# The first three second-pass heads one to an iteration, and the go of kept heads in groups of 3 and 3

## The chip, the cores and the metric

The kernel runs on one core of a Trainium2 chip. The metric is the time of one execution on the device in microseconds (us); lower is better. Three runs of the kernel before took 912.86, 911.12 and 912.86 us, a median of 912.86. A core has a matrix engine (TensorE, PE in the profile, its weight loads PEld), a vector engine (VectorE, DVE), a scalar engine (ScalarE, ACT), a general engine (GpSimd, POOL) and a sync engine (SyncE, SP). Here SP issues the loads, POOL the large stores and ACT some other stores. An engine executes its own instructions in the order in which they were written and waits for the others through semaphores.

## What is computed

The reference is one decode step of a transformer block, forward and backward, for B = 2 sequences of one token, model width D = 640, H = 32 heads, a cache of Sk = 4096 positions and head width 128, all in bfloat16:

```
q = layernorm(x) @ wq
p = softmax(q . k_cache * scale);  o = p . v_cache
h = x + o @ wo
out = h + relu(layernorm(h) @ w1) @ w2
```

Besides `out` it returns the gradients of a given `grad_out` by x, k_cache, v_cache, wq, wo, w1 and w2. The two caches have 2 x 32 heads of 1 MB each; both are read, and a gradient of the same size is written for each. The gradient of a V head is the outer product of p and go (go is the gradient by that head's o); the gradient of a K head is the outer product of gs and q, where gs needs go, V and p. So the gradients of a sequence need its forward pass through the MLP and back first, and V is needed a second time.

## The kernel before

**Two passes over the heads.** The order of all work is written out by hand: the program's loops issue instructions in the order in which every engine runs them. The first pass, `p1_iter` (L463), takes the 64 heads (32 of sequence 0, then 32 of sequence 1) in iterations i = 0 to 65. Iteration i transposes K of head i on PE (L416), copies the transposes out of PSUM (L421 on ACT), multiplies by q (L427) and ends in a maximum on DVE (`rmax`, L573). Beside this it multiplies K of head i-1 by its exponentials in two halves on DVE (`pk`, L478), and uses V of head i-2 in eight pieces on PE (`m_ps`, L471). K is given back after the second `pk`, V after the last piece of `m_ps`.

**Middle.** After head 31, `middle_gen` (L733) does sequence 0's attention output, layernorms, MLP and their gradients, in small pieces that run between the steps of first-pass iterations. At its end `go_group` (L672) makes go for a group of heads: one product on DVE for each head (`junk`, L658), then a few small operations on DVE and PE (L681 to L700). The groups stand in `bounds` (L802): for sequence 0, heads 26 and 27, heads 28 to 31, then 0 to 7 and so on.

**Second pass.** `p2_iter` (L837) takes head j of `turns` (L393): of each sequence its kept heads first, those whose V stayed in SBUF (six, heads 26 to 31, of sequence 0, and five of sequence 1), then the others, whose V is loaded again as `Wt` (L458). For a head it transposes V in pairs (L437, copied at L442 on ACT), multiplies by go (L450), writes the gradient of V as two halves (`gV`, L832, its store at L889), and, when the next head starts, gs (`gsp`, L845) and the gradient of K in two halves (`gK`, L832, its store at L870). Both stores are issued by POOL. Before head j starts, `bg_until` (L1058) makes sure that its go is there; if it were not, the rest of that group would be issued in one piece.

**The plan.** `plan` (L1070 to L1078) says which i and which j stand together. The second pass starts at i = P2_AT = 41 and has every second first-pass iteration (41, 43, ... 63), then every one. From i = 66 on it runs alone. In an iteration with both, five of a head's six steps stand between the first pass's steps (`MIXED`, L1120), and the last half of `gV` in the next iteration.

**Tiles of 1 MB.** Twelve tiles in SBUF serve as load targets (`ld`) and as sources of stores (`g`). `give` (L105) returns a tile; with a tag it changes the tile's use. `pump` (L1097) issues the next load of the queue as soon as an `ld` tile is free; which V of the second pass is loaded when follows from the plan (L1090). At i = 41 the tile of K goes from `ld` to `g` (L563), and `give` at L883 hands tiles of kept V to `g` until `g` has three.

Of the kernel before, what the change touches and what calls it, by code (L numbers as in the profile page):

```python
# [15 lines left out]
def kernel(  # L16
# [23 lines left out]
    _, H, Sk, Dh = A_k_cache.shape  # L40
# [64 lines left out]
    def give(t, to=None):  # L105
        tag, k, _ = home_of.pop(id(t))
        to = to or goes_to(tag)
        owned[tag] -= 1
        owned[to] += 1
        free[to] += 1  # L110
        homes[to].append(k)
        given_at[k] = step[0]
# [620 lines left out]
    def middle_gen(b):  # L733
        if o_next[0] < (b + 1) * H // OG:
            o_group()
        nc.vector.tensor_reduce(out=u4[:], in_=u_bank[0][:].rearrange("p (s d) -> p d s", s=4),
                                axis=AX.X, op=ALU.add)
        yield
        while a_next[0] < (b + 1) * H // OG:
            if a_next[0] == o_next[0]:  # L740
                o_group()
                yield
                yield
            a_group()
            yield
        at_bf = small.tile([128, ND], BF16, tag="at_bf", bufs=1, name="at_bf")
        nc.vector.tensor_copy(out=at_bf[:], in_=asum[:, b, :])
        nc.vector.tensor_tensor(out=h1c[:, :, b], in0=xg32[:, b, :], in1=at_bf[:], op=ALU.add)
        h32 = small.tile([128, 1, ND], FP32, tag="h32", bufs=1, name="h32")
        nc.vector.tensor_copy(out=h32[:, 0, :], in_=h1c[:, :, b])  # L750
        yield ("a", b)
        u_out(b)
        yield from ln_fwd(h32[:], 1, x2c[:, :, b:b + 1], rstd2[:, b:b + 1])
        hf_ps = pst([128, NF], FP32, "mid", "hf_ps")
        for cf in range(NF):
            kc = f_kc(cf)
            for c in range(ND):
                nc.tensor.matmul(hf_ps[0:kc, cf:cf + 1], lhsT=w1_t[:, c, cf * 128:cf * 128 + kc],
                                 rhs=x2c[:, c, b:b + 1], start=(c == 0), stop=(c == ND - 1))
            yield 0.25  # L760
        nc.vector.tensor_scalar(out=acol[:, 0:NFF, b], in0=hf_ps[:, 0:NFF], scalar1=0.0, scalar2=None, op0=ALU.max)
        if F_rem:
            nc.vector.tensor_scalar(out=acol[0:F_rem, NFF, b:b + 1], in0=hf_ps[0:F_rem, NFF:NF],
                                    scalar1=0.0, scalar2=None, op0=ALU.max)
        if b == B - 1:
            ar_ps = pst([128, NFF, B], FP32, "mid", "ar_ps")
            for cf in range(NFF):
                for c in range(ND):
                    nc.tensor.matmul(ar_ps[:, cf, :], lhsT=w1_t[:, c, bass.ds(cf, 128, step=NFF)],
                                     rhs=x2c[:, c, :], start=(c == 0), stop=(c == ND - 1))  # L770
                yield 0.25
            nc.vector.tensor_scalar(out=arow[:, 0:NFF, :], in0=ar_ps[:], scalar1=0.0, scalar2=None, op0=ALU.max)
            if F_rem:
                nc.vector.tensor_copy(out=arow[:, NFF, :], in_=acol[:, NFF, :])
        mask = small.tile([128, NF], FP32, tag="mask", bufs=1, name="mask")
        nc.vector.tensor_single_scalar(out=mask[:], in_=acol[:, :, b], scalar=0.0, op=ALU.is_gt)
        nc.vector.tensor_tensor(out=ghfc[:, :, b], in0=ga[:, b, :], in1=mask[:], op=ALU.mult)
        yield from wait(3)
        fbc = cols.tile([128, Dff], BF16, tag="fbc", name="fbc")
        gx2 = small.tile([128, 1, ND], FP32, tag="gx2", bufs=1, name="gx2")  # L780
        gx2p = small.tile([128, ND, 3], FP32, tag="gx2p", bufs=1, name="gx2p")
        FW = Dff // 3
        spread_f = bcast_cols(one(ghfc, b), NF, f_kc, fbc)
        have = 0
        for k in range(3):
            while have < min(Dff, (k + 1) * FW):
                next(spread_f)
                have += 512
                yield
            for c in range(ND):  # L790
                yield from turn()
                ttr(w1_t[:, c, k * FW:(k + 1) * FW], fbc[:, k * FW:(k + 1) * FW], gx2p[:, c, k:k + 1], FW)
                yield 0.85
        nc.vector.reduce_sum(out=gx2[:, 0, :], in_=gx2p[:], axis=AX.X)
        yield ("w1", b)
        yield from ln_bwd(gx2[:], x2c[:, :, b:b + 1], rstd2[:, b:b + 1], gc[:, :, b:b + 1], gh1c[:, :, b:b + 1], 1)
        hbc = cols.tile([128, D], BF16, tag="rowbc", name="hbc")
        yield from bcast_cols(one(gh1c, b), ND, lambda c: 128, hbc)
        yield ("gh1", b)

        first = H - KEPT[b]
        bounds = [(first, first + 2), (first + 2, H)] if b == 0 else [(first, H)]  # L802
        bounds += [(h, min(first, h + GH)) for h in range(0, first, GH)]
        for h0, h1 in bounds:
            yield from go_group(b, h0, h1, hbc)
        if b > 0:
            yield from mlp_out()
# [29 lines left out]
    def p2_iter(j, busy):  # L837

        c = S2[j] if j < NP1 else None
        p = S2[j - 1] if j >= 1 else None  # L840
        if p is not None:
            bp, hp = turns[j - 1]
            pair_matvec(p["dp"], p.pop("T3"), 3, gom[:, hp, bp, :, :])
            gsp = small.tile([128, NSC, 2], BF16, tag="gsp", name="gsp")
            nc.vector.scalar_tensor_tensor(  # L845
                out=gsp[:], in0=p["dp"][:, :, None].to_broadcast([128, NSC, 2]), scalar=negdot[:, hp, bp:bp + 1],
                in1=P_bf[:, bp * H + hp, :, None].to_broadcast([128, NSC, 2]), op0=ALU.add, op1=ALU.mult)
        if c is not None:
            b, h = turns[j]
            go = gom[:, h, b, :, :]  # L850

            bank = pst([128, 512], FP32, "sps", "dp_ps")
            for k, col in enumerate((goc, qsc)):
                nc.tensor.matmul(bank[:, 128 + k * 128:256 + k * 128],  # L854
                                 lhsT=col[:, h, b:b + 1].to_broadcast([128, 128]), rhs=ident_bf[:],
                                 start=True, stop=True)
            c["dp"] = bank[:, 0:NSC]
            rb = mats.tile([128, 256], BF16, tag="rb", bufs=4, name="rb")
            nc.scalar.activation(out=rb[:], in_=bank[:, 128:384], func=ACT.Copy, scale=rt[:, b, h:h + 1])  # L859
            pp = small.tile([128, NSC, 2], BF16, tag="pp", name="pp")  # L860
            nc.gpsimd.tensor_copy(out=pp[:], in_=P_bf[:, b * H + h, :, None].to_broadcast([128, NSC, 2]))
            c.update(rb=rb, pp=pp)
            c["T0"] = pair_transpose(c["W"], 0, busy=busy)
        if p is not None:
            gK = take("g", [128, NSC, 128], "gK")
            outer_half(gK, p["rb"][:, 128:256], gsp, 0)
        yield
        if p is not None:
            outer_half(gK, p["rb"][:, 128:256], gsp, 1)
            nc.gpsimd.dma_start(out=natural(out_2, bp, hp), in_=gK[:])  # L870
            give(gK)
            del S2[j - 1]
        yield
        if c is None:
            return
        c["T1"] = pair_transpose(c["W"], 1, busy=busy)
        pair_matvec(c["dp"], c.pop("T0"), 0, go)
        yield
        c["T2"] = pair_transpose(c["W"], 2, busy=busy)
        pair_matvec(c["dp"], c.pop("T1"), 1, go)  # L880
        yield
        c["T3"] = pair_transpose(c["W"], 3, busy=busy)
        give(c["W"], "g" if j < H and j != 1 and owned["g"] < 3 else None)  # L883
        pair_matvec(c["dp"], c.pop("T2"), 2, go)
        gV = take("g", [128, NSC, 128], "gV")
        outer_half(gV, c["rb"][:, 0:128], c["pp"], 0)
        yield
        outer_half(gV, c["rb"][:, 0:128], c["pp"], 1)
        nc.gpsimd.dma_start(out=natural(out_3, b, h), in_=gV[:])  # L889
        give(gV)  # L890
        yield
# [171 lines left out]
        forced[0] = False  # L1063

    M0_ITERS = 7
    P2_AT = H + 2 + M0_ITERS
    RATES = (0.2, 0.8, 0.2, 0.8, 0.45)
    RATE2 = 0.65
# [2 lines left out]
    i = j = 0  # L1071
    while i <= NP1 + 1 or j <= NP1:
        ii = i if i <= NP1 + 1 else None
        jj = j if i >= NP1 or (i >= P2_AT and (i - P2_AT) % 2 == 0) else None
        plan.append((ii, jj))
        i += 1
        if jj is not None:
            j += 1  # L1078
# [169 lines left out]
```

## Time and profile before

| | |
|---|---|
| median of three runs | 912.86 us (911.12 to 912.86) |
| profiled execution, first to last instruction (span) | 908.6 us |
| time around the span: median less span | 4.26 us |
| PE, DVE, ACT, POOL busy | 740.8, 692.1, 530.7, 173.1 us |
| bytes moved by DMA, mean rate | 363.00 MB, 400 GB/s |
| of these read from HBM, written to it | 212.16 MB, 149.13 MB |
| one load of K or V, issue to landing, median | 16.0 or 15.5 us |
| one store of gV or gK, issue to landing, median | 15.4 or 15.3 us |

The profiled execution has no time of its own beside its span; 4.26 us for what lies around it is the difference from the median. In the page's row of forty slices, a slice is 22.7 us. A row of the view by windows gives, for a stretch of time, the microseconds for which each engine was busy, the granted clock of PE, the mean busy share of the sixteen DMA engines, and the rate at which bytes moved. The timeline gives start and length of single instructions. A DMA's issue has its line on the issuing engine; its landing is a time of its own.

### The profile page before, as it was taken

Reading aid. Unit: us, or ns where it says so; the run is one execution under the profiler, and the core shown is the slowest. Engines: PE = TensorE matmul, PEld = TensorE weight load, DVE = VectorE, ACT = ScalarE, POOL = GpSimd, SP = SyncE. Lnnn points to the kernel's source line nnn. Section 1 sums busy time; section 2 is a strip of 40 time slices with the busy share of each in tenths; the row PEclk is TensorE's granted clock in tenths of the full one; section 3 lists DMA queues with packets and bytes.
Section 4 is the critical chain, followed back from the end, with each engine's and each line's share of the span. In section 5 each row is a group of like instructions: output and inputs, shape, how many; then the busy total and the mean of one; then the engine's idle time right before and its main releaser. Section 6 shows DMA issues by size and latency. Waiting matters only on the chain.

```text
span 908.6 us, 26495 instructions
## 1 busy us (share of the span) xinstructions
PE 740.8 (82%) x11227; PEld 620.3 (68%) x11227; DVE 692.1 (76%) x1282; ACT 530.7 (58%) x1096; POOL 173.1 (19%) x329
## 2 busy tenths in 40 slices
PE   3899999999989898997866844886799778949780
PEld 3788888888878787887765844665667566735560
DVE  2565787877879787786879697986798459899982
ACT  1666665567777777675743443654577656537650
POOL 1232223323201111010011111121222111111120
PEclk9999999999999999898997585655557555555655
DMA  9999999999889999999999999999999999999996
GB/s 364 420 409 404 408 399 409 418 419 362 308 296 339 421 420 423 422 422 420 417 388 406 412 425 413 402 400 392 397 400 389 424 425 425 423 427 425 425 422 261
DMA packets 56262, 363.00 MB, mean 400 GB/s; under 512 B 5680, under 2 KB 11696, under 8 KB 15312
## 3 DMA queue, kind: packets, MB, share of 16 engines
q1 hardware_dynamic: 34704, 212.18, 57.9%
q0 software_dynamic: 18432, 134.23, 35.6%
q10 hardware_dynamic: 3008, 14.91, 4.1%
q8 instruction: 88, 1.44, 0.6%
q14 instruction: 30, 0.25, 0.1%
HBM read 212.16 MB, written 149.13 MB: 398 GB/s over the span
## 4 chain that ended last, share of the span: by engine, by line
PE 36%; DMA 27%; DVE 18%; ACT 9%; issue 7%; POOL 0%; SPq 0%; POOLq 0%; ACTq 0%; DVEq 0%
DMA out_dram<-gK 11%; DMA Vt<-in_A_v_cache_dram 10%; PE m_ps L471 9%; PE t_ps L416 8%; PE t_ps L437 6%; DVE gV L832 5%; ACT t_sb L421 4%; DVE gK L832 4%; PE s_ps L427 4%; DVE junk L658 3%; PE u_ps L500 3%; DMA wqs<-in_A_wq_dram 3%; DMA out_dram<-gV 2%; DVE pk L478 2%; DMA Kt<-in_A_k_cache_dram 2%
## 5 line engine op out<-in xcount | busy, mean ns | idle before, releaser
L421 ACT COPY t_sb<-t_ps 128x1024 bf16<-128x1024 bf16 x223 | 217.8, 1018 | 45.6 <-PE t_ps L416 45.3
L442 ACT COPY t_sb<-t_ps 128x512 f32<-128x512 f32 x256 | 149.8, 588 | 132.0 <-PE t_ps L437 128.9
L478 DVE TENSOR_TENSOR pk<-Kt,ep 128x2048 bf16<-128x2048 bf16 x128 | 156.3, 1221 | 57.9 <-ACT ep L526 29.1
L437 PE MATMUL t_ps<-ident_f,Wt 128*128 128x128 f32 x848 | 190.9, 371 | 1.0 <-ACT t_sb L421 1.0
L471 PE MATMUL m_ps<-pk,Vt 128*128 128x129 bf16 x2048 | 171.3, 222 | 11.7 <-DMA Vt<-in_A_v_cache_dram 10.3
L832 DVE TENSOR_TENSOR gK<-rb,gsp 128x2048 bf16<-128x2048 bf16 x128 | 152.5, 1225 | 22.2 <-DMA out_dram<-gV 20.4
L832 DVE TENSOR_TENSOR gV<-rb,pp 128x2048 bf16<-128x2048 bf16 x128 | 153.0, 1219 | 20.9 <-DMA out_dram<-gK 18.0
L416 PE MATMUL t_ps<-ident_bf,Kt 128*128 128x128 bf16 x2048 | 152.3, 223 | 8.2 <-DMA Kt<-in_A_k_cache_dram 2.3
L437 PEld LDWEIGHTS t_ps<-ident_f,Wt 128*128 128x128 f32 x848 | 131.4, 191 | 32.4 <-issue 26.1
L471 PEld LDWEIGHTS <-Vt 128*128 128x128 bf16 x2048 | 125.0, 99 | 41.4 <-issue 30.0
L416 PEld LDWEIGHTS <-Kt 128*128 128x128 bf16 x2048 | 125.2, 100 | 16.3 <-issue 10.4
L450 PEld LDWEIGHTS <-t_sb 128*128 128x128 bf16 x2048 | 95.7, 106 | 44.4 <-issue 18.8
L450 PE MATMUL dp_ps<-gom,t_sb 128*128 128x2 bf16 x2048 | 95.1, 167 | 9.2 <-ACT t_sb L442 8.0
L488 POOL COPY pk<-ep 128x16 bf16<-128x16 bf16 x80 | 64.9, 812 | 188.2 <-ACT ep L526 159.9
L427 PE MATMUL s_ps<-qc,t_sb 128*128 128x1 bf16 x2048 | 88.1, 164 | 1.6 <-DVE t_sb L419 0.8
L889 POOL DMA_DIRECT2D out_dram<-gV x64 | 34.3, 536 | 277.0 <-DVE gV L832 198.3
L870 POOL DMA_DIRECT2D out_dram<-gK x64 | 34.1, 533 | 253.6 <-DVE gK L832 196.5
L427 PEld LDWEIGHTS <-t_sb 128*128 128x128 bf16 x2048 | 77.5, 97 | 4.4 <-ACT t_sb L421 1.2
L942 ACT CAST ot<-o_ps 128x512 bf16<-128x512 f32 (+4 forms) x160 | 70.3, 489 | 13.7 <-DMA out_dram<-ot 9.3
L859 ACT ACTIVATE rb<-dp_ps,rt 128x256 bf16<-128x256 f32 x64 | 30.4, 476 | 59.8 <-PE dp_ps L854 58.5
L585 ACT CAST MT<-m_ps 128x128 bf16<-128x128 f32 x64 | 17.1, 268 | 72.8 <-PE m_ps L471 72.7
L658 DVE CUSTOM_DVE_ANT_0 junk<-wo_t,hbc 128x640 bf16<-128x640 bf16 x64 | 52.4, 818 | 0.2
(197 smaller groups left out, 781.0 us busy)
## 6 DMA issues: line engine op xcount, KB each, us to landing
Kt<-in_A_k_cache_dram SPq DMA_DIRECT2D x64, 1024.0 KB, 16.0
Vt<-in_A_v_cache_dram SPq DMA_DIRECT2D x64, 1024.0 KB, 15.5
out_dram<-gV POOLq DMA_DIRECT2D x64, 1024.0 KB, 15.4
out_dram<-gK POOLq DMA_DIRECT2D x64, 1024.0 KB, 15.3
Wt<-in_A_v_cache_dram SPq DMA_DIRECT2D x53, 1024.0 KB, 14.0
wq_t<-in_A_wq_dram SPq DMA_DIRECT2D x5, 1024.0 KB, 8.9
wo_t<-in_A_wo_dram SPq DMA_DIRECT2D x4, 1280.0 KB, 18.7
wqs<-in_A_wq_dram SPq DMA_DIRECT2D x5, 1024.0 KB, 17.2
```

The lines of the kernel that those rows point to most:

```text
L416: nc.tensor.transpose(t_ps[:, j, :], nat[:, g * GT + j, :], ident_bf[:])
L421: nc.scalar.copy(out=t_sb[:], in_=t_ps[:])
L427: nc.tensor.matmul(dst[:, sc:sc + 1], lhsT=t_sb[:, j, :], rhs=vec, start=True, stop=True)
L437: nc.tensor.transpose(t_ps[:, j, :], natf[:, 2 * cc:2 * cc + 2, :].rearrange("p c k -> p (c k)"), ident_f[:])
L442: nc.scalar.copy(out=t_sb[:], in_=t_ps[:])
L450: nc.tensor.matmul(dst[:, sc:sc + 2], lhsT=v[:, j, :, par], rhs=vecs[:, par, :], start=(par == 0), stop=(par == 1))
L471: nc.tensor.matmul(r["m"][:, 0:129], lhsT=r["V"][:, sc, :], rhs=r["pk"][sc // HALF][:, sc % HALF, 0:129], start=(sc == 0), stop=(sc == NSC ...
L478: nc.vector.tensor_tensor(out=p["pk"][k][:, :, 0:128].rearrange("p s (a two) -> p s a two", two=2), in0=p["K"][:, sl, :].rearrange("p s (a ...
L488: nc.gpsimd.tensor_copy(out=col, in_=e)
L658: nc.vector.tensor_tensor_reduce(out=junk[0:kc, 0:width], in0=in0, in1=in1, scale=1.0, scalar=0.0, op0=ALU.mult, op1=ALU.add, accum_out=acc)
L832: nc.vector.tensor_tensor(out=pairs_view(dst[:, sl, :]), in0=row.rearrange("p (a two) -> p a two", two=2)[:, None, :, :].to_broadcast([128 ...
L942: nc.scalar.copy(out=ot[0:P, k, n0:n0 + nn], in_=o_ps[0:P, 0:nn])
```

## The change

The plan gets a constant RAMP = 3: the second pass also runs at i = 42. Its heads stand at i = 41, 42, 43, 45, 47, ... 63, then at every i, so that before i = 66 it has begun fifteen heads (j = 0 to 14) instead of fourteen; the plan has 116 iterations instead of 117. The first two go groups of sequence 0 become heads 26 to 28 and 29 to 31. In `p2_iter` the head whose kept V does not go to `g` is j = 2 instead of j = 1.

```diff
@@ middle_gen @@
         first = H - KEPT[b]
-        bounds = [(first, first + 2), (first + 2, H)] if b == 0 else [(first, H)]
+        bounds = [(first, first + 3), (first + 3, H)] if b == 0 else [(first, H)]
@@ p2_iter @@
         c["T3"] = pair_transpose(c["W"], 3, busy=busy)
-        give(c["W"], "g" if j < H and j != 1 and owned["g"] < 3 else None)
+        give(c["W"], "g" if j < H and j != 2 and owned["g"] < 3 else None)
@@ plan @@
     M0_ITERS = 7
+    RAMP = 3
     P2_AT = H + 2 + M0_ITERS
...
-        jj = j if i >= NP1 or (i >= P2_AT and (i - P2_AT) % 2 == 0) else None
+        jj = j if i >= NP1 or (i >= P2_AT and ((i - P2_AT) % 2 == 0 or i < P2_AT + RAMP)) else None
```

## Prediction

> **What bounds the kernel now.** I read the forty slices first, then the place of the change in windows of 5 us, then its iterations, then single issues.
>
> ```profile
> DMA  9999999999889999999999999999999999999996
> GB/s 364 420 409 404 408 399 409 418 419 362 308 296 339 421 420 423 422 422 420 417 388 406 412 425 413 402 400 392 397 400 389 424 425 425 423 427 425 425 422 261
> ```
>
> The rate says more than the busy share: most slices move 400 to 427 GB/s, so for most of the span the kernel waits for bytes. The exception is slices 9 to 12 (204 to 295 us), at 296 to 362. The second pass starts inside them: the first rb (L859) stands at 265.4 us. By windows of 5 us:
>
> ```profile
> 270.00:275.00 5.00, 4.95 (x98) 4.63 (x95) 4.34 (x8) 3.62 (x9) 0.00 (x0) 1.00 0.60 192
> 275.00:280.00 5.00, 4.55 (x93) 3.92 (x90) 4.90 (x15) 4.24 (x9) 1.69 (x2) 1.00 0.80 285
> 280.00:285.00 5.00, 4.22 (x79) 3.58 (x79) 4.36 (x10) 4.18 (x9) 0.53 (x1) 1.00 0.97 387
> 285.00:290.00 5.00, 4.82 (x102) 4.67 (x100) 3.82 (x10) 2.74 (x7) 0.00 (x0) 1.00 1.00 365
> 290.00:295.00 5.00, 5.00 (x99) 4.28 (x97) 5.00 (x12) 4.05 (x10) 1.70 (x2) 1.00 0.96 333
> 295.00:300.00 5.00, 3.03 (x59) 2.81 (x58) 3.16 (x6) 3.27 (x8) 0.00 (x0) 1.00 1.01 416
> 300.00:305.00 5.00, 4.34 (x84) 3.80 (x83) 3.17 (x6) 2.88 (x6) 0.53 (x1) 1.00 1.01 421
> ```
>
> The last column fills up at 295 us. Against 421 GB/s the four rows from 275 to 295 lack 136, 34, 56 and 88 GB/s: 314 x 5 us = 1.57 MB, or 3.7 us of transfer. The same iterations (41, 42, 43 and 44, cut near their rmax) and two later stretches:
>
> ```profile
> 264.00:272.00 8.00, 7.07 (x126) 6.11 (x125) 4.28 (x12) 5.92 (x12) 0.00 (x0) 1.00 0.73 275
> 272.00:278.00 6.00, 5.95 (x120) 5.13 (x119) 6.00 (x10) 5.43 (x13) 1.69 (x2) 1.00 0.79 283
> 278.00:287.00 9.00, 7.77 (x159) 7.01 (x156) 7.46 (x20) 6.60 (x13) 0.53 (x1) 1.00 0.97 366
> 287.00:295.00 8.00, 7.82 (x152) 6.96 (x149) 7.62 (x20) 6.04 (x14) 1.70 (x2) 1.00 0.98 336
> 690.00:890.00 200.00, 159.58 (x1440) 116.91 (x1438) 162.16 (x231) 120.23 (x255) 31.69 (x68) 0.57 1.01 422
> 300.00:450.00 150.00, 133.69 (x2437) 118.32 (x2436) 117.89 (x238) 107.18 (x221) 16.44 (x27) 0.94 1.01 422
> ```
>
> Up to 295 us the engines bound it (iteration 42 has DVE busy all 6.00 of 6.00 us and PE 5.95); from 300 on the bytes do, at 422 GB/s in both long stretches. So I count in two currencies: before 295 us an instruction costs time, after it a byte does. The stores and loads concerned:
>
> ```profile
> 275.36 0.69 POOL L889 DMA_DIRECT2D out_dram<-gV  x1 [13.49 <-DVE gV L832]
> 282.82 0.53 POOL L870 DMA_DIRECT2D out_dram<-gK  x1 [5.78 <-DVE gK L832]
> 291.74 0.53 POOL L889 DMA_DIRECT2D out_dram<-gV  x1 [8.38 <-DVE gV L832]
> 300.46 0.53 POOL L870 DMA_DIRECT2D out_dram<-gK  x1 [7.02 <-DVE gK L832]
> ```
>
> They landed 5.2, 8.1, 10.2 and 8.9 us after issue. The rmax of iterations 40 to 45 start at 263.6, 271.6, 278.4, 287.3, 294.6 and 304.4 us: an iteration with a second-pass head lasts 8.0 (i = 41) or 8.9 us (43), one without 6.8 (42) or 7.3 (44).
>
> **What the change moves.** No operation on a head goes away; one more head stands before i = 45. Head 1 runs in iteration 42 instead of 43, head 2 in 43 instead of 45, and every later one a place earlier. When the full stretch begins, 2 x 1.049 MB of stores more are under way. At 421 GB/s that is 4.98 us of later transfer time: the **credit**. It can't exceed what the holes have room for, 3.7 us, plus what a late first pass opens.
>
> **Cost 1, the head's work in iteration 42.** On DVE it brings gsp 0.28, two gK of 1.225 and, of its gV, nearly one half more than before. Next to each other in the timeline such instructions take less than their length: from the start of a gV to its successor is 1.14 us, from a junk of 0.82 to its reader 0.74. Iteration 42 would hold two gV halves 2.28, one junk with its reader 0.9, nb 0.2, gsp 0.3, two gK 2.3, two pk 2.3 and rmax, OU and OFc 0.3: 8.6 us in place of 6.8. Rows of mixed iterations give 8.0 and 8.9, so 1.2 to 2.1 more; I take 1.8. PE gets 16 transposes (4 pieces of 0.66) and 4 pieces of 0.34 for the products, about 4 us; it was full too, and both run in parallel. Iterations 43 and 44 keep the same load with another head: nothing.
>
> **Cost 2, a new wait of DVE for a tile.** With one head after the other, the two g tiles come round at once. Stepping through take and give: gV of head 0 uses K's tile, gK of head 0 the first kept V; gV of head 1 takes K's again, gK of head 1 the first V's again, since the tile that head 1 hands over stands behind them. By the sums above, gV of head 0 is issued near 275.1 and its tile wanted near 280.2; landing after 5.2 us it is free. gK of head 0 is issued near 277.9 and its tile wanted near 283.8; landing after 5.2 to 8.1 us it comes free at 283.1 to 286.0. The wait is 0 to 2.2 us; I take the middle, 1.1. Behind the waiting gK in DVE's queue stand both pk of iteration 43, behind them on SP the next load of K, and on PE m_ps. If all landed after 10.2 us the waits would add up to some 7 us.
>
> **Costs at nothing.** The group of three go has one more junk (0.82 us) before i = 41; it takes the place of one of the second group, and stepping through the loop shows each group of sequence 0 finished in an earlier iteration than the head that needs it. The second (heads 29 to 31) and the third (0 to 7) are done just in the iteration before; that is the cover, and without it up to three junks, 2.5 us, would go out in one piece. Loads: the three g tiles are complete at i = 42 instead of 45, and head 2 returns its tile to ld instead; counting the tiles that come free, the loads issued by the end of i = 44 are the same number and at i = 45 one more. SP has its first V of the second pass a place earlier among K and V; POOL has the same sequence of stores. The middle of sequence 1 starts at the same i and is always ahead of its heads; the end is byte-bound (421 GB/s and a store landing 14.7 us after issue), which hides that the last gradient work stands one head nearer the end.
>
> **Sum.** Credit 4.98 - 1.8 - 1.1 = 2.1 us, with ends 4.98 - 1.2 = 3.7 (also the whole hole) and 4.98 - 2.1 - 2.2 = 0.7. The profiled span of 908.6 would become 906.5; with the 4.26 us between span and median, **910.8 us** against 912.86.
>
> **Two rules against it.** POOL's gK and gV are issued while DVE is busy; the store issued at 291.74, in a window with DVE busy 5.00 of 5.00, landed after 10.2 us, the one at 275.36 after 5.2, so a busy DVE alone does not decide. The Trainium skill (SBUF — State Buffer, summary of rules for kernel authors) says that descriptor generation for stores from GpSimd starves while VectorE runs in its fast modes. By that rule the stores of heads 0 and 1 would come only with DVE's next pause, and the credit would shrink to about nothing. The same section tells to reckon with some 358 GB/s for HBM. By that figure the rows at 285 and 333 alone lack anything, 0.5 MB or an estimated 1.4 us as a bound; the rows at 421 and 422 contradict it here.
>
> **Rivals.** *The waits win (slower).* If gV and gK of head 1 wait more than 3.2 us together, slip exceeds credit. With gV waiting 5.1 us (a landing of 10.2 instead of 5.2, wanted 5.1 us after its issue) the slip is 6.9 and the time 914.8. For it: landings of 8 to 10 us right after. Against it: at 278 only one load is outstanding. *The gain is given back.* The stretches 450 to 460, 460 to 470 and 485 to 490 run at 368, 390 and 344 GB/s, holes of 3.0 us where the passes part; with another head there they may grow by two thirds: 912.9. *The head is free.* The second pass alone takes (884.5 - 485.1) / 48 = 8.3 us a head and the plan has one iteration less; if only the 1.8 us of iteration 42 were paid, 906.4. Against it: 422 GB/s from 300 to 450 us leaves no room for the shifted bytes.
>
> **Chances.** Forecast 0.50, of which 0.32 lie over 0.2% (1.8 us, about what a measurement can tell from no change) below before; waits 0.22; given back 0.18; free 0.10. So faster 0.42, same 0.36, slower 0.22. The range from 906.8 to 915.2 takes in the forecast's ends and the waits' price; it leaves out most of the free head and waits beyond 5.5 us.
>
> **What would show it.** After: rmax of iteration 42 near 280 and of 45 near 307 us; windows from 280 to 295 at 400 or more; gK of head 1 waiting for out_dram on DVE 0 to 2 us; 422 still from 300 to 450; rb of head 12 some 4 us before its 459.4 us, since it stands at i = 63 then. Wrong: windows from 280 to 300 as empty as before, waits of DVE over 3 us there, or a lower rate after 450 us.

## The result, and the profile after

The changed kernel takes **918.04 us** (median of 11 runs, 915.67 to 922.44) against 912.86 (median of 11 runs, 910.53 to 915.50): a ratio of 1.0059, 95% interval 1.0043 to 1.0075. It is slower, where 910.8 was forecast. The profiled execution has a span of 914.5 us (908.6 before). Its own time is 916.29 us.

The page's rows of forty slices, now 22.9 us each:

```profile
DMA  9999999999779999999999999999989999999997
GB/s 365 420 409 403 408 402 409 419 415 369 291 279 376 371 424 422 422 420 423 422 401 362 422 422 423 420 388 382 394 340 366 424 425 417 424 423 425 425 424 303
```

Slices 9 to 12 (counted from 0) stood at 362, 308, 296 and 339 before and at 369, 291, 279 and 376 now. They are hardly fuller, the next slice fell from 421 to 371, and there is a hole that was not there: the thirtieth figure, 340, and the 366 behind it (663 to 709 us; 400 and 389 before). Four stretches by windows show how much each weighs; the last column is GB/s. First the kernel before:

```profile
270.00:320.00 50.00, 44.82 (x867) 40.03 (x865) 41.45 (x84) 36.88 (x77) 6.70 (x9) 1.00 0.94 367
320.00:650.00 330.00, 257.81 (x3800) 223.45 (x3798) 265.20 (x496) 185.63 (x392) 49.92 (x96) 0.77 1.01 411
650.00:710.00 60.00, 52.67 (x499) 39.96 (x498) 51.78 (x87) 41.74 (x94) 14.85 (x24) 0.61 0.99 397
710.00:880.00 170.00, 135.50 (x1173) 97.85 (x1172) 139.29 (x193) 101.16 (x216) 26.12 (x56) 0.54 1.01 425
```

The same windows of the changed kernel:

```profile
270.00:320.00 50.00, 43.88 (x808) 38.97 (x801) 40.42 (x78) 34.55 (x73) 7.77 (x11) 0.97 0.91 344
320.00:650.00 330.00, 251.24 (x3833) 217.17 (x3832) 263.95 (x487) 183.05 (x387) 50.55 (x94) 0.80 1.01 412
650.00:710.00 60.00, 47.58 (x457) 36.96 (x456) 47.53 (x83) 35.64 (x83) 10.56 (x22) 0.55 0.91 358
710.00:880.00 170.00, 135.98 (x1228) 97.02 (x1226) 138.08 (x191) 105.70 (x230) 27.18 (x56) 0.59 1.01 423
```

Both kernels move 363.00 MB. At the place of the change the kernel now moves (367 - 344) x 50 = 1.15 MB less, 2.7 us at 421 GB/s; it should have moved more. From 650 to 710 us it lacks another (397 - 358) x 60 = 2.34 MB, 5.6 us, 350 us away from the change. The two other rows differ by 0.8 us each, in opposite directions. Part of the 8.3 us comes back behind 880 us, where the old kernel moved only 294 GB/s and the new one 344; 5.9 us of span remain. So there are two losses to explain, a **near** one and a **late** one.

The near one by windows of 5 us:

```profile
270.00:275.00 5.00, 4.97 (x98) 4.46 (x91) 3.44 (x6) 2.87 (x8) 0.00 (x0) 1.00 0.29 74
275.00:280.00 5.00, 4.18 (x80) 3.38 (x78) 4.97 (x7) 4.59 (x10) 2.03 (x3) 1.00 0.84 349
280.00:285.00 5.00, 4.97 (x96) 4.73 (x94) 4.51 (x10) 3.19 (x7) 0.00 (x0) 1.00 0.98 352
285.00:290.00 5.00, 4.22 (x78) 3.50 (x77) 4.96 (x8) 3.86 (x9) 2.02 (x3) 1.00 0.99 393
290.00:295.00 5.00, 4.95 (x110) 4.70 (x108) 3.86 (x10) 3.48 (x9) 0.00 (x0) 1.00 1.02 411
295.00:300.00 5.00, 4.62 (x87) 3.83 (x84) 4.79 (x16) 3.32 (x9) 1.49 (x2) 1.00 1.01 351
300.00:305.00 5.00, 1.38 (x20) 1.32 (x21) 1.35 (x5) 1.50 (x3) 0.00 (x0) 0.91 0.99 403
305.00:310.00 5.00, 5.00 (x78) 4.43 (x77) 3.40 (x5) 3.82 (x8) 0.53 (x1) 0.74 1.01 419
310.00:315.00 5.00, 4.96 (x99) 4.63 (x97) 4.27 (x8) 3.69 (x9) 0.00 (x0) 1.00 1.00 375
315.00:320.00 5.00, 4.62 (x93) 4.00 (x91) 4.87 (x13) 4.22 (x9) 1.71 (x2) 1.00 0.95 310
```

The hole of before, 275 to 295 us, is partly filled: 349, 352, 393 and 411 against 285, 387, 365 and 333, together 0.68 MB more. But 270 to 275 us fell from 192 to 74, and 295 to 300 us and 310 to 320 us are new holes. Between 300 and 305 us PE and DVE are busy for 1.4 of 5 us each: something holds both.

The starts of rmax give the length of each first-pass iteration (us):

| iteration | 40 | 41 | 42 | 43 | 44 | 45 | 46 | rmax 45 starts at |
|---|---|---|---|---|---|---|---|---|
| before | 7.0 | 8.0 | 6.8 | 8.9 | 7.3 | 9.9 | 6.8 | 304.4 |
| after | 7.2 | 9.2 | 9.3 | 9.7 | 6.9 | 12.9 | 6.8 | 311.6 |

By these lengths the first pass loses 0.2 us in iteration 40, 1.1 in 41, 2.5 in 42, 0.8 in 43, -0.4 in 44 and 3.1 in 45, 7.3 us in all (by the starts before rounding). The stores came earlier by 4.98 us of transfer. The difference, 2.3 us, is close to the 2.7 of the windows. The link between the two is argued: a first pass that is late by so much gives its tiles back late, and its loads are issued late.

What holds PE and DVE in iteration 45 stands in the chain of waits (start, us, what; one part of it):

```profile
291.73 0.51 PE t_ps L437 x4
...
292.26 10.93 DMA Vt<-in_A_v_cache_dram
...
303.24 0.64 PE m_ps L471 x8
```

PE's last transpose of a kept V sets a tile free at 292.24, the load of V of head 43 goes into it, lands 10.93 us later, and m_ps had waited for it. Before, the same link reads:

```profile
287.79 8.79 DMA Vt<-in_A_v_cache_dram
```

The wait was there already (PE's timeline of the kernel before):

```profile
296.63 0.64 PE L471 MATMUL m_ps<-pk,Vt 128*128 128x129 bf16 x8 [1.60 <-DMA Vt<-in_A_v_cache_dram]
```

Now the load is issued 4.5 us later and takes 2.1 us longer, and PE waits 3.37 us. The wait is not the whole of it. Behind it PE's granted clock is lower: 0.74 (the third figure from the end) from 305 to 310 us in the windows above. In the kernel before (first row) it is 1.00 there, in a second execution of the changed kernel (second row) 0.50:

```profile
305.00:310.00 5.00, 4.95 (x96) 4.12 (x93) 5.00 (x10) 4.97 (x11) 1.71 (x2) 1.00 1.01 426
305.00:310.00 5.00, 4.62 (x58) 4.50 (x57) 3.84 (x5) 2.48 (x6) 0.53 (x1) 0.50 0.97 403
```

At the lower clock PE takes longer for the same work: four transposes of V last 1.06 us at 304.60 against 0.60 at 297.93 before. So of the 3.1 us more in iteration 45, 1.8 are the longer wait and the rest comes behind it. The first theory was therefore: *the near loss is engine work plus a contention of that load with the stores of heads 1 and 2*; its rival, *the wait of DVE for store tiles*. For the late loss: *what is switched on j now comes an iteration too early*, against *it follows from the near loss*, since a later first pass makes everything later.

### The profile page after: what moved, and what is told of

Its sections match the earlier page's. It is cut to its first block, busy times and chain, and to the rows that moved or that the text cites. A ratio compares the mean times of both kernels' runs of the same rounds, so it can differ in the third digit from the quotient of the medians.

```text
span 914.5 us, 26491 instructions
## 1 busy us (share of the span) xinstructions
PE 733.3 (80%) x11227; PEld 612.4 (67%) x11227; DVE 692.1 (76%) x1282; ACT 527.6 (58%) x1096; POOL 174.9 (19%) x329
## 2 busy tenths in 40 slices
DMA packets 56262, 363.00 MB, mean 397 GB/s; under 512 B 5680, under 2 KB 11696, under 8 KB 15312
## 4 chain that ended last, share of the span: by engine, by line
PE 38%; DMA 26%; DVE 19%; ACT 9%; issue 7%; SPq 0%; POOL 0%; ACTq 0%; POOLq 0%; DVEq 0%
DMA Vt<-in_A_v_cache_dram 12%; PE m_ps L471 9%; PE t_ps L416 8%; PE t_ps L437 7%; DVE gV L832 5%; DVE gK L832 5%; DMA wqs<-in_A_wq_dram 4%; ACT t_sb L421 4%; DMA out_dram<-gK 4%; DMA out_dram<-gV 4%; PE s_ps L427 4%; DVE junk L658 3%; PE u_ps L500 3%; DVE gxj L658 2%; PE o_ps L936 2%
## 5 line engine op out<-in xcount | busy, mean ns | idle before, releaser
L437 PE MATMUL t_ps<-ident_f,Wt 128*128 128x128 f32 x848 | 184.9, 361 | 2.6 <-ACT t_sb L421 2.6
L437 PEld LDWEIGHTS t_ps<-ident_f,Wt 128*128 128x128 f32 x848 | 127.2, 186 | 37.1 <-issue 30.6
L942 ACT CAST ot<-o_ps 128x512 bf16<-128x512 f32 (+4 forms) x160 | 70.2, 491 | 20.5 <-DMA out_dram<-ot 14.1
## 6 DMA issues: line engine op xcount, KB each, us to landing
out_dram<-gV POOLq DMA_DIRECT2D x64, 1024.0 KB, 12.9
out_dram<-gK POOLq DMA_DIRECT2D x64, 1024.0 KB, 12.9
Wt<-in_A_v_cache_dram SPq DMA_DIRECT2D x53, 1024.0 KB, 14.6
```

What stands on the lines that cost most here:

```text
L437: nc.tensor.transpose(t_ps[:, j, :], natf[:, 2 * cc:2 * cc + 2, :].rearrange("p c k -> p (c k)"), ident_f[:])
L942: nc.scalar.copy(out=ot[0:P, k, n0:n0 + nn], in_=o_ps[0:P, 0:nn])
```

## The experiments

Each line is a ratio of times to the kernel before, measured beside it on the same chip, with its 95% interval; behind it the rates (GB/s) of its one profiled execution in the two stretches. "Later" means that both switches on j described below come one head later.

| kernel | ratio | 270 to 320 us | 650 to 710 us |
|---|---|---|---|
| before | 1 | 367 | 397 |
| the change | 1.0059 (1.0043 to 1.0075) | 344 | 358 |
| the change again | 1.0085 (1.0060 to 1.0110) | 334 | 373 |
| e1 the change, later | 1.0062 (1.0039 to 1.0085) | 339 | 387 |
| e2 before, switches one head earlier | 1.0034 (1.0016 to 1.0053) | 367 | 378 |
| e3 before, go groups 3 and 3 | 1.0020 (1.0004 to 1.0036) | 351 | 389 |
| e4 before, one more head at i = 54 | 1.0039 (1.0019 to 1.0059) | 366 | 365 |
| e5 the change, head 1's tile to ld | 1.0084 (1.0059 to 1.0110) | 328 | 368 |
| e7 before, later | 1.0005 (0.9982 to 1.0027) | 368 | 403 |
| e8 the change, four stores left out | one run, 915.68 us | 300 | 366 |
| e9 before, q tiles later | 1.0007 (0.9983 to 1.0031) | 363 | 399 |
| e10 e4, later | 1.0005 (0.9978 to 1.0031) | 361 | 397 |
| e11 the change, later, q tiles later | 1.0066 (1.0042 to 1.0091) | 340 | 389 |
| e12 before, one more head at i = 44, later | 1.0011 (0.9988 to 1.0035) | 352 | 399 |
| e13 the change, later, groups 2, 1 and 3 | 1.0068 (1.0044 to 1.0092) | 334 | 386 |
| e15 e4, rates later only | 0.9993 (0.9977 to 1.0010) | 367 | 387 |
| e16 e4, hand-over later only | 1.0012 (0.9995 to 1.0030) | 369 | 389 |

Single executions of one kernel differ by several us (before: 908 to 918), so ratios carry the verdicts, and a trace is read for what stands at its place in all of them.

**The change again.** No edit; it shows which parts of the difference repeat.

> The changed kernel once more, to see which holes of its trace come back. Keyed theory (the later background work is switched by the head's number j, so a second pass that is one head ahead gets its slow background rate and its tile hand-over one plan iteration earlier, and the stretch with few load tiles lasts longer): about 918 us, the load queue again stands still for some 45 us around 655 to 700 us, against 38 us before, and the windows from 660 to 700 us run near 350 GB/s. Rival (the weak stretch at 660 to 700 us was chance of one execution): about 918 us, but the hole stands elsewhere or is gone in this trace.

Both losses repeat. The lengths of iterations 41 to 44 are the same to 0.1 us; iteration 45 lasts 15.2 instead of 12.9 us, with a load of V of 12.10 us, a wait of 3.51 and the clock of 0.50 shown above. The late loss is there too (373 for 397). Iteration 45 is the one of these lengths that differs between executions: in the four traces with the changed kernel's heads, go groups and tiles (the two, e1 and e11) it lasts 12.9, 15.2, 14.6 and 13.8 us, in the eight with the old ones (the kernel before, e2, e4, e7, e9, e10, e15, e16) 9.1 to 11.9. By the means, 14.1 and 10.0, it costs 4.1 us; the pair of traces read above shows less.

### The near loss

**e3: the go groups alone.**

```diff
-        bounds = [(first, first + 2), (first + 2, H)] if b == 0 else [(first, H)]
+        bounds = [(first, first + 3), (first + 3, H)] if b == 0 else [(first, H)]
```

> The kernel before with only the go groups of 3 and 3 (heads 26 to 28, 29 to 31). Theory: the third go ahead of the first second-pass head delays iteration 41 by about 1.1 us in the stretch that the engines bound, so 913.5 to 914.2 us, rmax of iteration 41 near 272.7 us. Rival as predicted blind (hidden): 912.9 us, rmax of 41 at 271.6 us.

It costs 0.20% (0.04 to 0.36), 1.8 us. Iteration 41 lasts 9.2 us, as in the changed kernel, with nothing else of the change there. PE's timeline of e3 (start, us, engine, line; in brackets the idle time before and what ended it):

```profile
263.93 0.34 PE L427 MATMUL s_ps<-qc,t_sb 128*128 128x1 bf16 x8
265.48 0.35 PE L688 MATMUL d_ps<-pr,ones_f32c 128*128 128x3 f32 x2 [1.21 <-DVE gom L342]
265.69 0.21 PE L692 MATMUL d_ps<-goc,MT 128*128 128x1 bf16 x3
```

Before, the product at L688 had no wait, with 2 columns for two heads:

```profile
262.59 0.36 PE L688 MATMUL d_ps<-pr,ones_f32c 128*128 128x2 f32 x2
```

The third junk makes DVE reach the group's small operations later, and PE, which executes in order, stands 1.21 us at d_ps with the transposes of the next first-pass head behind it. So the third go, costed at nothing, costs the whole of iteration 41's slip.

**e13: the first group of two kept, then one, then three** (on e1).

```diff
-        bounds = [(first, first + 3), (first + 3, H)] if b == 0 else [(first, H)]
+        bounds = [(first, first + 2), (first + 2, first + 3), (first + 3, H)] if b == 0 else [(first, H)]
```

> The changed kernel with the switches on j one head later, and the go of kept heads in groups of 2, 1 and 3 (heads 26 and 27, 28, 29 to 31): head 28 is done in iteration 41 or 42, so no third go stands in front of the first second-pass head, and the ramp is kept. Theory (the third go costs 1.2 us of iteration 41): iteration 41 lasts 8.0 us, 915.5 to 917 us against 917 to 918.5 with three. Rival (the wait moves to another iteration): iteration 41 lasts 8.0, but 42 or 43 is longer by as much, and the time is as with groups of 3 and 3.

No gain: the small operations then run once more. Iteration 41 lasts 10.4 us (42: 8.9, 45: 15.0), and now DVE waits for PE:

```profile
272.14 0.16 DVE L694 TENSOR_SCALAR negdot<-d_ps 128x1 f32<-128x1 f32 x1 [3.01 <-PE d_ps L692]
```

With one group more in this stretch there is one wait more, whatever the number of heads in it.

**e8: the four stores of heads 1 and 2 left out** (on the changed kernel; everything else stays).

```diff
+            if j - 1 not in (1, 2):
-            nc.gpsimd.dma_start(out=natural(out_2, bp, hp), in_=gK[:])
+                nc.gpsimd.dma_start(out=natural(out_2, bp, hp), in_=gK[:])
...
+        if j not in (1, 2):
-        nc.gpsimd.dma_start(out=natural(out_3, b, h), in_=gV[:])
+            nc.gpsimd.dma_start(out=natural(out_3, b, h), in_=gV[:])
```

> The changed kernel without the four stores of second-pass heads 1 and 2 (4.2 MB of the gradients of K and V are not written); nothing else is left out. Only iterations 42 to 46 are read from it. Theory (the loads of K and V lose the transfer to these stores): iteration 45 takes 9 to 10 us instead of 12.9 to 15.2, and PE does not wait for V there. Rival (loads are late because their tiles come free late): iteration 45 still 12 us or more.

Iterations 42 and 43 last 9.3 and 9.7 us as with the stores; these are engine work. Iteration 45 lasts 8.7 instead of 12.9 us. PE's timeline of the changed kernel:

```profile
299.66 0.22 PE L517 MATMUL s_ps<-neg_ident,rmax 128*128 128x128 bf16 x1
303.24 0.64 PE L471 MATMUL m_ps<-pk,Vt 128*128 128x129 bf16 x8 [3.37 <-DMA Vt<-in_A_v_cache_dram]
```

The same place in e8, whose first pass runs 1.3 us later as a whole:

```profile
300.58 0.22 PE L517 MATMUL s_ps<-neg_ident,rmax 128*128 128x128 bf16 x1
300.79 0.64 PE L471 MATMUL m_ps<-pk,Vt 128*128 128x129 bf16 x8
```

Without the stores PE does not wait for V, though the load (at 293.59) is issued as late against its iteration as in the changed kernel: it landed within 7.2 us, by the m_ps at 300.79, where it took 10.93. The clock stays at 1.00. That the wait in iteration 45 comes from a load slowed beside these stores is shown in this one execution, which is shorter there than any other. It leaves out four stores, two more than the change brings in. What it brings to the end is little: 4.2 MB fewer are 10.0 us at 421 GB/s, the one run took 915.68 us, 2.4 under the changed kernel's median. In its trace 650 to 710 us runs at 366 again. As far as one run can tell, bytes saved here are not worth their transfer time at the end.

**e5: head 1 gives its tile back to ld and head 2 to g** (the third edit of the change undone).

```diff
-        give(c["W"], "g" if j < H and j != 2 and owned["g"] < 3 else None)
+        give(c["W"], "g" if j < H and j != 1 and owned["g"] < 3 else None)
```

> The changed kernel with the condition j != 1 kept, so that the V tile of the second kept head goes back to the loads and that of the third to the stores. The load of V that iteration 45 waits for then has a tile some 1.7 us earlier. Theory (iteration 45 waits for V because its load is issued too late): iteration 45 takes 10 to 12 us instead of 12.9 to 15.2, 915 to 917 us. Rival (it is late because the stores of heads 1 and 2 share the transfer with it): iteration 45 as long as before, 918 us. Second rival (with two store tiles, gV of head 2 waits for a store to land): DVE waits for out_dram 1 to 3 us in iteration 43 or 44.

The load of V goes out earlier, at 290.70 instead of 292.26, but now g lacks a tile, and DVE waits (timeline of e5):

```profile
296.48 1.23 DVE L832 TENSOR_TENSOR gV<-rb,pp 128x2048 bf16<-128x2048 bf16 x1 [4.38 <-DMA out_dram<-gV]
```

Iteration 44 grows from 6.9 to 12.6 us, and 45 shrinks from 12.9 to 10.4. A ratio of 1.0084 (1.0059 to 1.0110) is no better than the changed kernel's. The wait moved to the other kind of tile. This is the mechanism of the rival "the waits win"; the third edit of the change keeps it out.

**e12: one more head at i = 44, old go groups, later** (the kernel before, with this edit and the three edits of e7 below).

```diff
-        jj = j if i >= NP1 or (i >= P2_AT and (i - P2_AT) % 2 == 0) else None
+        jj = j if i >= NP1 or (i >= P2_AT and ((i - P2_AT) % 2 == 0 or i == P2_AT + 3)) else None
```

> The extra head at i = 44 instead of 42 (second-pass heads at i = 41, 43, 44, 45, 47, ...), with the go groups of 2 and 4 of the kernel before, and the switches on j one head later. Iteration 41 then lasts 8.0 us again (no third go in front of it). Theory (local sum: credit 4.98 us against the head's work of some 2.5 us and a longer wait for V): cumulative bytes at 330 us within 2 us of transfer of before, better than the changed kernel by 1.4 us or more; time 912 to 915 us. Rival (the burst of stores always ends in a late load of V): rmax of iteration 46 still 4 us or more behind, and bytes at 330 us 2 to 4 us behind.

The lead is the same, two iterations later, and no loss can be measured (1.0011, 0.9988 to 1.0035). Iterations 41 to 43 have their old lengths, 44 lasts 9.8 (7.3 before), 45 15.3 us. That long iteration has the other cause: DVE waits for a store to land, and with it nb and all that stands behind.

```profile
302.77 1.23 DVE L832 TENSOR_TENSOR gV<-rb,pp 128x2048 bf16<-128x2048 bf16 x1 [4.27 <-DMA out_dram<-gV]
```

So a third head inside these iterations stalls either PE for V or DVE for a tile, wherever it is put. Against e1 (1.0062) it saves the go group's 1.1 us and some engine work. But its first pass is 7.9 us late behind iteration 45, counted from the rmax of 40, against 7.1 in the changed kernel and 8.7 in e1, as its rival had it. So the lateness of the first pass does not by itself give the time, and why e12 is 0.5% better than e1 stays open.

### The late loss

In the second pass alone the program reads j in two places. The pace at which the middle of sequence 1 runs beside the heads falls from 0.8 to 0.45 after j = H, with fewer slots a head; and from j = H + KEPT[1] - 1 the large tiles are handed over to g, q and f (`share`, at L1147 and L1148 of the kernel before). With one head more begun, both come one iteration of the plan earlier, while the middle itself is started by i. Stepping through the loop shows load tiles down to five for five iterations of the plan (91 to 95) instead of three (92 to 94).

**e2 and e7: the kernel before, with the switches one head earlier and one later.** e2:

```diff
-        elif fin is not None and j >= H + KEPT[1] - 1:
+        elif fin is not None and j >= H + KEPT[1] - 2:
...
-                      2 if i is not None else 3 if j <= H else 4]
+                      2 if i is not None else 3 if j <= H - 1 else 4]
...
-                slot[0] = int(k in ((1, 3, 5) if j <= H else (1, 4)))
+                slot[0] = int(k in ((1, 3, 5) if j <= H - 1 else (1, 4)))
```

> The kernel before, its plan untouched, with the same three switches one head earlier (j <= H - 1, hand-over from j = 35). Keyed theory: slower by some 5 us, 917 to 919 us, with the load queue still for some 45 us. Rival (the loss comes from the ramp or from chance): 912.9 us.

> The kernel before, its plan untouched, with the three switches on j one head later than they are (both j <= H become j <= H + 1, hand-over from j = 37). Keyed theory, if a later switch goes on helping: 910 to 912 us, windows from 660 to 710 us at 400 GB/s or more. If before already has the best place: 912 to 914 us.

e7 has `j >= H + KEPT[1]` and `j <= H + 1` (twice) at the same places. Earlier costs 0.34% (0.16 to 0.53) with no change at all near 300 us; later changes nothing (0.9982 to 1.0027). A loss there does not need the near one. Five load tiles last five iterations of the plan in e2, as in the changed kernel, and two in e7.

**e4, e10, e15, e16: a lead of one head without the near stretch.** e4 puts one more head at i = 54, into the 422 GB/s; the others undo one or both switches on top of it.

```diff
-        jj = j if i >= NP1 or (i >= P2_AT and (i - P2_AT) % 2 == 0) else None
+        jj = j if i >= NP1 or (i >= P2_AT and ((i - P2_AT) % 2 == 0 or i == P2_AT + 13)) else None
```

> The kernel before with one more second-pass head, but at i = 54, in the stretch that runs at 422 GB/s, and with its own go groups: the lead of one head without the ramp near 300 us. Keyed theory (a lead of one head alone costs later, through the switches on j, and in a full stretch it buys nothing): 915 to 917 us, windows from 660 to 710 us at 355 to 380 GB/s instead of 397, nothing lost before 450 us. Rival (the loss is all in the ramp): 912 to 913 us.

> The run with the extra head at i = 54, and now also the switches on j one head later. Keyed theory: of the 3.9 us that the lead of one head cost there, most comes back: 912 to 913.5 us, windows from 660 to 710 us at 389 to 400 GB/s instead of 359. Rival (the lead costs elsewhere, where the two passes part): still 915 us or more, 660 to 710 us full again and 450 to 510 us at 384 GB/s instead of 401.

> The run with the extra head at i = 54, with only the background's rate and slots switched one head later; the hand-over of tiles stays at j = 36. If the slower go is what the lead costs: 912 to 913.5 us and windows from 660 to 710 us at 385 to 400 GB/s. If the hand-over is: 915 us and 360 GB/s as without it.

> The run with the extra head at i = 54, with only the hand-over of tiles one head later; rates and slots switch as in it. If the hand-over is what the lead costs: 912 to 913.5 us and windows from 660 to 710 us at 385 to 400 GB/s. If the slower go is: 915 us and 360 GB/s as without it.

e10 has e7's three edits, e15 only the two with `j <= H + 1`, e16 only `j >= H + KEPT[1]`. The lead costs 0.39% with the switches coupled to it, and nothing that can be measured with them moved: 1.0005, 0.9993 and 1.0012, intervals within 0.9977 to 1.0031. Moving either switch alone seems enough. For the rates (e15) no loss is left; for the hand-over (e16) this is less certain, since its interval (0.9995 to 1.0030) overlaps e4's (1.0019 to 1.0059). Stepping through the loop, five load tiles last five iterations in e4, four in e15 and e16, three in e10. The window from 660 to 710 us of e4:

```profile
660.00:710.00 50.00, 44.11 (x409) 33.91 (x407) 39.64 (x68) 32.71 (x76) 8.32 (x19) 0.54 0.89 359
```

The same of e10, both switches moved:

```profile
660.00:710.00 50.00, 45.46 (x446) 36.02 (x446) 44.27 (x75) 34.88 (x80) 12.73 (x21) 0.59 1.00 399
```

Of e15, the rates alone:

```profile
660.00:710.00 50.00, 45.28 (x422) 34.22 (x421) 45.72 (x76) 34.53 (x80) 11.68 (x21) 0.59 0.96 385
```

And of e16, the hand-over alone:

```profile
660.00:710.00 50.00, 44.69 (x428) 35.38 (x425) 42.91 (x72) 34.48 (x78) 12.30 (x21) 0.57 0.98 388
```

e4 shows the changed kernel's hole (357 in the same 50 us there) at full size, with the near stretch untouched (366 for 367 GB/s from 270 to 320 us). DVE does fewer operations (68 instead of 72 to 76), and the DMA engines are busy for 0.89 of the time. The lead itself, taken where the rate was full already, buys nothing that can be measured either: 0.9993 (0.9977 to 1.0010) is the best of the four, and of all kernels here. No version tried is faster than the kernel before. (e10's profiled execution took 918.99 us, its median is 911.81; its trace is read for this stretch only.)

**e1: the change with both switches later.**

```diff
-        elif fin is not None and j >= H + KEPT[1] - 1:
+        elif fin is not None and j >= H + KEPT[1]:
...
-                      2 if i is not None else 3 if j <= H else 4]
+                      2 if i is not None else 3 if j <= H + 1 else 4]
...
-                slot[0] = int(k in ((1, 3, 5) if j <= H else (1, 4)))
+                slot[0] = int(k in ((1, 3, 5) if j <= H + 1 else (1, 4)))
```

> The changed kernel with the three switches that look at j moved one head on (both j <= H become j <= H + 1, the tile hand-over starts at j = 37), so that they come at the same plan iteration as before the change. Keyed theory: the 5 to 6 us lost between 660 and 710 us come back and the local loss of 2 to 3 us near 300 us stays: 912 to 914 us; load queue still for some 38 us. Rival (chance, or the head lead itself): 918 us as without it. Rival (all of the loss is the ramp near 300 us): 918 us.

The hole is mostly gone from the trace (387 GB/s from 650 to 710 us instead of 358 and 373), the time is not: 1.0062 (1.0039 to 1.0085) against 1.0085 (1.0060 to 1.0110) for the changed kernel beside it and 1.0059 in the first measurement. The intervals overlap; a recovery of 0.3% is neither shown nor excluded. So in the changed kernel itself the switches have not been shown to be the larger part. In e1's execution the near stretch was also among the worse ones (iteration 45 took 14.6 us, and 339 GB/s).

**e9 and e11: the q tiles later**, on the kernel before and on e1. The queue of loads (SP) stands still in this stretch, and a hand-over that leaves more tiles to ld first should shorten it.

```diff
-            share(ld=5 + more, g=5 + 2 * more, f=3, q=2 + 3 * more)
+            share(ld=7 - more, g=5 + 2 * more, f=3, q=5 * more)
```

> The kernel before with one change in the hand-over of tiles from j = 36 on: the loads keep 7 tiles instead of 5 until all go of sequence 1 are made, and the q tiles, which nothing uses before that, come only then. Theory (the weak stretch from 660 to 700 us comes from loads that stand still for want of tiles): the load queue stands still for 15 to 25 us instead of 38 us, windows from 660 to 710 us at 405 GB/s or more, 909.5 to 911.5 us against 912 to 913. Rival (the stretch is bound by the work on DVE and PE beside it, the loads only follow): rate and time as before.

> The changed kernel with the switches on j one head later and the hand-over of the q tiles only when all go are made. Theory: nothing is left lost after 650 us; what stays are the 2 to 5 us near 300 us and what the parting of the passes takes: 914 to 916 us. Rival: 917 us or more, as with the switches alone.

The waits of SP's queue from 620 to 720 us (us in total, times, longest), first in the kernel before:

```profile
SPq L458 <- PE t_ps L437: 74.2, 5, 37.9
```

In the changed kernel:

```profile
SPq L458 <- PE t_ps L437: 91.6, 6, 44.7
```

In e9:

```profile
SPq L458 <- PE t_ps L437: 46.3, 5, 12.3
SPq L458 <- PE dp_ps L450: 38.4, 3, 22.3
```

The longest standstill grew from 37.9 to 44.7 us with the change, which looked like the cause. e9 cuts it to 22.3, and neither the rate (399 for 397) nor the time (1.0007, 0.9983 to 1.0031) follows; e11 (longest standstill also 22.3 us) stays at 1.0066. So the standstill of before costs nothing that can be measured. Whether the longer one causes the hole is not tested: e9 and e11 start from kernels that do not have the hole, or hardly, and no run gives e4 or the changed kernel more load tiles. In e15 the standstill is 42.3 us, at 387 GB/s and without a loss.

## Why the prediction was wrong, point by point

**What bounds the kernel: right up to 450 us, and read too short.** Up to 295 us engines, from 300 to 450 bytes, held. But in the old kernel PE already waited 1.60 us for V in iteration 45, on a load that took 8.79 us. The prediction read this iteration's end (304.4) and not what it waited for.

**Credit, 4.98 us: the stores came, their worth did not.** Windows from 280 to 295 us were to be at 400 or more and are at 352, 393 and 411; 0.68 of the missing 1.57 MB were filled. The ceiling "the hole, plus what a late first pass opens" was in the text; the sum took all of the 4.98 all the same. It also priced a byte moved early at its full transfer time up to the end; in e8's one run 10.0 us of bytes fewer brought 2.4.

**Cost 1, 1.8 us in iteration 42: mis-sized, and it ended too early.** It measured 2.5 us. DVE's timeline of the changed kernel (the iteration reaches from 272.78 to 282.05):

```profile
272.89 1.23 DVE L832 TENSOR_TENSOR gV<-rb,pp 128x2048 bf16<-128x2048 bf16 x1
274.03 0.82 DVE L658 CUSTOM_DVE_ANT_0 junk<-wo_t,hbc 128x640 bf16<-128x640 bf16 x1
...
274.77 1.22 DVE L832 TENSOR_TENSOR gV<-rb,pp 128x2048 bf16<-128x2048 bf16 x1
...
276.42 2.46 DVE L832 TENSOR_TENSOR gK<-rb,gsp 128x2048 bf16<-128x2048 bf16 x2
278.81 1.21 DVE L478 TENSOR_TENSOR pk<-Kt,ep 128x2048 bf16<-128x2048 bf16 x1
...
282.05 0.19 DVE L573 TENSOR_REDUCE rmax<-s_ps 128x1 bf16<-128x32 f32 x1 [0.46 <-PE s_ps L427]
...
284.04 1.22 DVE L832 TENSOR_TENSOR gV<-rb,pp 128x2048 bf16<-128x2048 bf16 x1
```

The parts are those of the prediction's list, nearly back to back as it said. What it left out are the 0.46 us for PE at the end and the small copy of P_bf. **"Iterations 43 and 44 keep the same load: nothing" failed**: both halves of a head's gV come behind the next rmax. Iteration 43 of before held no gV, since 42 had no head; now it holds two (282.16 and 284.04), 2.3 us, and loses the end of a go group and a wait of 0.56. It is 0.8 us longer.

**Cost 2, the wait of DVE for a tile: did not occur.** From 264 to 320 us DVE waits for no out_dram. POOL's timeline of the changed kernel:

```profile
276.31 0.69 POOL L889 DMA_DIRECT2D out_dram<-gV  x1 [14.38 <-DVE nb L519]
...
279.19 0.53 POOL L870 DMA_DIRECT2D out_dram<-gK  x1 [1.39 <-DVE gK L832]
...
285.55 0.53 POOL L889 DMA_DIRECT2D out_dram<-gV  x1 [5.83 <-DVE nb L519]
...
288.42 0.53 POOL L870 DMA_DIRECT2D out_dram<-gK  x1 [1.38 <-DVE gK L832]
```

They landed after 4.4, 5.6, 8.3 and 8.9 us. gK of head 1 started at 285.69, behind the landing of head 0's gK at 284.8. So the rival "the waits win" had the sign, by luck: its time (914.8) was 3.2 us short, and its mechanism did not occur; e5 and e12 show that it stood one tile or one iteration away (4.38 and 4.27 us).

**"Costs at nothing: the third go junk" failed.** Finished in time was the wrong question; PE's in-order wait behind it (1.21 us) is what costs, 1.1 us in iteration 41 and 0.20% alone (e3).

**"Costs at nothing: loads" failed in iteration 45.** The count of loads up to iteration 44 was right (eight from 263 us on, in both traces); but the one that PE waits for goes out later by the slip and lands later beside two heads' stores, and PE runs at a lower clock behind the wait: 3.1 us more in iteration 45, gone in e8. This is the largest term of the near loss and has none in the sum.

**The near sum by its measured terms**: 4.98 - 0.2 - 1.1 - 2.5 - 0.8 + 0.4 - 3.1 = -2.3 us, where +2.1 was predicted; with the 4.1 us that iteration 45 costs by the means, -3.4. The 4.98 in it is the prediction's own price.

**"The middle of sequence 1 starts at the same i and is always ahead of its heads" was not enough.** The pace and the hand-over of tiles hang on j; earlier by one head they cost 0.34% (e2) or, with a lead, 0.39% (e4).

**"The gain is given back" at 450 to 490 us: not settled.** From 450 to 510 us the changed kernel moves 392 for 401 GB/s and the four with a head at i = 54 370 to 390, but so does e2 (388) without such a head, and from 510 to 600 us all of them move more than before (415 to 420 for 408). In the changed kernel there was no gain left to give back: rb of head 12, forecast near 455, came at 458.4. **The head is free**: refuted by iterations 41 to 45. From 300 to 450 us the mean was 416 for 422 GB/s, all of it lost before 320.

**The rule on starving store descriptors**: the store issued at 276.31, in a window with DVE busy 4.97 of 5.00 us, landed after 4.4 us. The starving that the Trainium skill states (SBUF — State Buffer, summary of rules for kernel authors) does not show in this store.

**The time around the span**: the changed kernel's eleven runs have spans 1.8 to 1.9 us below their own times, not 4.26; the other 2.3 to 2.5 us, worked out, were the place of the profiled execution among the runs. Adding them back to the median was harmless here.

**What stays open.** Alone, the go groups cost 0.20% and the earlier switches 0.34%; with the near loss this makes up the 0.6 to 0.85% in size, but the parts do not subtract one by one: e1 removes most of the hole and not the time, and e12 has a first pass as late as the changed kernel's and no measurable loss. How the 5.2 us of the changed kernel divide into near and late is therefore not shown. What in the two switches slows 650 to 710 us is not settled beyond "either one moved seems enough". What lowers PE's clock in iteration 45 is not settled either: it is below 1.00 behind every wait for V of 3.1 us or more, but also in e2, e9 and e10 with waits of 1.2 to 1.9.

## What to carry to other kernels

A head moved forward pays where it goes, at once and in order: follow each small operation behind it on PE's and DVE's queue, and the next load's landing beside the new stores, before its bytes are credited. A wait can cost more than its length: read the granted clock behind it. Before moving work by an index, search for everything that compares that index, however far away; here two switches, met 350 us later, cost 0.34% when moved alone. Bytes moved early can be credited in full only if every later stretch is bound by bytes; in e8's one run they were not worth their transfer time.

## What the runs showed of the hardware

The busy share of the sixteen DMA engines does not tell how full they are: at 0.99 to 1.02 the changed kernel moved 393, 411, 351 and 403 GB/s from 285 to 305 us, against 424 in full stretches. A load of 1.049 MB took 8.79 us before, 10.93 and 12.10 us in two executions beside the stores of heads 1 and 2, and at most 7.2 us with these left out.

In iteration 45, behind a wait of PE of 3.37 us, its granted clock was 0.54 and 0.61 in the 4 us from 304 us on, where it was 1.00 in the kernel before.
